# An attention and mixture-of-experts kernel: one-hot routing rows by comparing logits with the two largest, and q and k rotated in one VectorE operation

## The chip, the cores and the metric

The kernel runs on one core of one Trainium2 chip. The metric is the device time of one execution in microseconds (us). The profile shows five engines of that core: PE (TensorE: matmuls, with PEld for its weight loads), DVE (VectorE), ACT (ScalarE), POOL (GpSimd) and SP (SyncE, which here only issues DMA transfers). Each engine takes its instructions in the order in which they stand; engines wait for each other through semaphores.

## The reference

```python
def _attn_ref(q, k, v, a_re, a_im):            # B=4, H=8, S=768, D=48
    mag = np.sqrt(a_re * a_re + a_im * a_im)
    scale = np.minimum(mag, 0.999) / (mag + 1e-06)
    a_re_n, a_im_n = (a_re * scale, a_im * scale)
    for t in range(S):                         # complex state S, D x D per head
        S_re, S_im = (ar * S_re - ai * S_im + kv, ar * S_im + ai * S_re)
        y[:, :, t] = einsum('bhd,bhde->bhe', q[:, :, t], S_re)

def _moe_ref(x, w_gate, w_noise, noise, w1, w2):   # N=3072, D=384, E=8, F=1024
    noisy_logits = x @ w_gate + np.log1p(np.exp(x @ w_noise)) * noise
    top2 = np.argpartition(-noisy_logits, 2, axis=1)[:, :2]
    top2_w = softmax over the two logits
    out[row] = sum over its two experts e of weight * (relu(x @ w1[e]) @ w2[e])
```

The output of the attention, put in rows of 384, is the input x of the mixture of experts.

## The kernel before, in words

**Attention.** The sequence is cut into 24 tiles of 128 positions (6 stretches g of the sequence times 4 batches b). The decay of the state is taken out of the recurrence: its magnitude multiplies q and k (line 280, `qk` by `ee`), its phase turns them. `p3q` does the turning for one tile: q (i = 0) and k (i = 1) are each multiplied by the cosine and the sine rows `tr`, in one operation of 768 elements per partition each (line 288), into `qh` and `kh`. There are two buffers of each (`NQ = 2`), so tile n+2 writes over tile n. Then `tr_unit` transposes the eight heads of q, later those of k, on PE into the one PSUM tile `ptr` (line 298), and ACT copies them out as `qT` and `kT` (line 299); `sc_unit` makes the scores `psc` in two halves (307) and DVE masks each into `am` (308); `st_unit` adds k times v to the state in `pG` (317), which reads `kh` directly; `y_unit` makes the output `pY` from state and scores (354, 356), which ACT copies to `xT` (357).

**Gating.** `gate_logits` makes the logits of a group of tiles, `gates` turns them into weights: `softplus`, the eight largest logits of each row sorted (`max`, line 57, one for each tile), the positions of these (`max_index`, line 59, which the trace shows as MATCH_VALUE_LOAD and FIND_INDEX8), one-hot rows `oh` by comparing the positions with 0 to 7 (line 61), softmax weights. `gate_dispatch` counts the rows of each expert on PE (405, 407, from `ohs`, line 400) and POOL scatters each row to its slots (421). The groups are four of 4 tiles (`ga4`), two of 3 (`ga3`) and two of 1 (`ga1`).

**Experts.** Eight experts follow with w1 and w2 split in high and low parts (`load_w1`, `load_w2`, 494, 495), `mm1` (557, 559, 563) and `mm2` (606, 617), whose results POOL scatters (618). A flag says whether the fast way was valid; where it was not, slower code (`slow_attention`, `dense_experts`) runs instead.

**Order.** Each unit is given a step by hand (the table `P` and `at`); within that priority a scheduler places the instructions on the engines, so a change of one operation can move others.

Of the kernel before, what the change touches and what calls it, by code (L numbers as in the profile page):

```python
# [9 lines left out]
F32 = mybir.dt.float32  # L10
F32R = mybir.dt.float32r
BF16 = mybir.dt.bfloat16
U32 = mybir.dt.uint32
I32 = mybir.dt.int32
AF = mybir.ActivationFunctionType
OP = mybir.AluOpType
AX = mybir.AxisListType
# [27 lines left out]
    return c  # L45


def gates(nc, pool, lz, noise, iota8, n, tag, act, g):


    nl = softplus(nc, pool, lz[:, :, 8:16], [128, n, 8], tag, act)
    nc.vector.tensor_mul(nl, nl, noise)
    nc.vector.tensor_add(nl, nl, lz[:, :, 0:8])
    mx = pool.tile([128, n, 8], F32, name=tag + "mx")
    ix = pool.tile([128, n, 8], U32, name=tag + "ix")
    for j in range(n):
        nc.vector.max(mx[:, j, :], nl[:, j, :])
    for j in range(n):
        nc.vector.max_index(ix[:, j, :], mx[:, j, :], nl[:, j, :])
    oh = pool.tile([128, 2, n, 8], F32, name=tag + "oh")  # L60
    nc.vector.tensor_tensor(oh, iota8[:, None, None, :].to_broadcast([128, 2, n, 8]),
                            ix[:, :, 0:2, None].rearrange("p n k o -> p k n o").to_broadcast([128, 2, n, 8]),
                            op=OP.is_equal)
    w = pool.tile([128, 2, n], F32, name=tag + "w2")
    e = pool.tile([128, n], F32, name=tag + "e")
    nc.vector.tensor_sub(e, mx[:, :, 1], mx[:, :, 0])
    act(w[:, 1], e, AF.Exp)
    nc.vector.tensor_scalar(e, w[:, 1], 1.0, 1e-9, op0=OP.add, op1=OP.add)
    nc.vector.reciprocal(w[:, 0], e)
    nc.vector.tensor_mul(w[:, 1], w[:, 1], w[:, 0])  # L70
    t = pool.tile([128, 2, n, 8], F32, name=tag + "t")
    nc.vector.tensor_mul(t, oh, w[:, :, :, None].to_broadcast([128, 2, n, 8]))
    nc.vector.tensor_add(g, t[:, 0], t[:, 1])
    return oh
# [3 lines left out]
def kernel(  # L78
# [8 lines left out]
    nc = tc.nc  # L87
# [3 lines left out]
    D = HD // H  # L91
    N, DM = out.shape
    E = w_gate.shape[1]
# [6 lines left out]
    NQ = 2  # L100
# [38 lines left out]
    iota8 = cp.tile([128, E], F32, name="iota8")  # L139
    nc.gpsimd.iota(iota8, pattern=[[1, E]], base=0, channel_multiplier=0,  # L140
                   allow_small_or_imprecise_dtypes=True)
    base_run = cp.tile([128, E], F32, name="base_run")
# [21 lines left out]
    pa = ap.enter_context(tc.tile_pool(name="pa", bufs=1, side="right"))  # L164
# [9 lines left out]
    nc.gpsimd.memset(wg, 0.0)  # L174
    nz = cp.tile([128, NG, B, E], F32, name="nz")

    qh = [pa.tile([128, H, 2, 64], F32, name=f"qh{i}") for i in range(NQ)]
    kh = [pa.tile([128, H, 2, 64], F32, name=f"kh{i}") for i in range(NQ)]
    for t in qh + kh:
        nc.gpsimd.memset(t[:, :, :, D:], 0.0)  # L180
    ecol = [pa.tile([112, B, H], F32, name=f"ecol{i}") for i in range(3)]
    for t in ecol:
        nc.vector.memset(t, 1.0)
# [7 lines left out]
    QT, KT, AM, Z, XR, QKD = {}, {}, {}, {}, {}, {}  # L191
# [91 lines left out]
        for r in range(2):  # L283
            nc.sync.dma_start(ec[64 * r:64 * r + D, b, :], es[n].rearrange("(h d) -> d h", h=H))

    def p3q(n, i):
        tr = TR[n // 2][:, :, n % 2, :].rearrange("p r (h d) -> p r h d", h=H)
        nc.vector.tensor_mul((qh, kh)[i][n % NQ][:, :, :, 0:D].rearrange("p h r d -> p r h d"),
                             QK[n][:, i, :].rearrange("p (h d) -> p h d", h=H)[:, None].to_broadcast([128, 2, H, D]),
                             tr)  # L290

    def tr_unit(n, i):
        x = (qh, kh)[i][n % NQ]
# [100 lines left out]
    def gate_dispatch(g, lo, hi, lz):  # L394
        n = hi - lo
        oh = gates(nc, pa, lz, nz[:, g, lo:hi], iota8, n, f"ga{n}",
                   lambda *a: phase(2 * min(g + 3, NG), *a),
                   XR[g][:, lo:hi, DM:DM + E])
        ohs = pa.tile([128, n, E], BF16, name=f"ohs{n}")
        nc.vector.tensor_add(ohs, oh[:, 0], oh[:, 1])  # L400
        p = psC.tile([128, 512], F32, name="cum")
        for j in range(n + 1):
            o = p[:, j * E:(j + 1) * E]
            for i in range(min(j, n)):
                nc.tensor.matmul(o, ones_b, ohs[:, i, :], start=(i == 0), stop=(j == n and i == n - 1))
            if j < n:
                nc.tensor.matmul(o, tri_b, ohs[:, j, :], start=(j == 0), stop=True)
        pos = pa.tile([128, n, E], F32, name=f"pos{n}")
        nc.vector.tensor_add(pos, p[:, :n * E].rearrange("p (b e) -> p b e", b=n),
                             base_run[:, None, :].to_broadcast([128, n, E]))  # L410
        nc.vector.tensor_add(base_run, base_run, p[:, n * E:(n + 1) * E])
        if g == NG - 4:
            nc.vector.tensor_copy(ncnt, base_run[:, 0:2])
        nc.vector.tensor_mul(oh, oh, pos[:, None].to_broadcast([128, 2, n, E]))
        sl = pa.tile([128, 2, n], U32, name=f"sl{n}", bufs=2)
        with nc.allow_low_precision("whole numbers"):
            nc.vector.tensor_reduce(sl, oh, axis=AX.X, op=OP.add)
        nc.sync.dma_start(xd[(g * B + lo) * C:(g * B + hi) * C].rearrange("(b s) r -> s b r", b=n), XR[g][:, lo:hi, 0:DM + E])
        for b in range(n):
            for kk in range(2):  # L420
                d = nc.gpsimd.indirect_dma_start(  # L421
                    out=xs, out_offset=bass.IndirectOffsetOnAxis(ap=sl[:, kk, b:b + 1], axis=0),
                    in_=XR[g][:, lo + b, :], in_offset=None, bounds_check=E * N - 1, oob_is_err=False)
                for s in scat:
                    tc.declare_no_dep(d.ins, s.ins, reason="slots differ")
                scat.append(d)

                n_y = PACE.get((g, lo + b))
                if n_y is not None:
                    behind.append((d, n_y))  # L430
# [4 lines left out]
    def at(step, f, *a):  # L435
        fill.setdefault(step, []).append((f, a))
# [190 lines left out]
    for g in range(NG):  # L627
        f = B * g + .5
        q1, q2, q3 = P.get(f"s{g}", (P["p1"], P["p2"], P["p3"]))
        for j in range(B // 2):  # L630
            m = B * g // 2 + j
            at(f - P["la"] if g else -20, load_a, m)
            at(f - q1 + j * P["d1"], p1, m)
            at(f - q2, p2a, m)
            at(f - q2, p2carry, m)
            at(f - q2 + .01, p2s, m)
        for j in range(B):
            n = B * g + j
            at(f - P["lqk"] if g else -14, load_qk, n)
            at(f - q2 + j * P["dt"], p2t, n)  # L640
            at(f - q3 + j * P["d3"] if n > 1 else f - q2 - .25, p3, n)
            for i in range(2):
                at(n + .5 - P["q"] + i * P["qd"] if n > 1 else f - q3, p3q, n, i)
    for n in range(NT):
        at(n + .5 - P["lv"], load_v, n)
        for i in range(2):
# [99 lines left out]
    nc.vector.tensor_add(ncnt[:, 0:1], ncnt[:, 0:1], ncnt[:, 1:2])  # L746
    flg = mp.tile([128, 2], F32, name="flg")
    nc.vector.tensor_reduce(flg[:, 0:1], bad.rearrange("p x g -> p (x g)"), axis=AX.X, op=OP.add)
    nc.vector.tensor_reduce(flg[:, 1:2], lim, axis=AX.X, op=OP.add)
    nc.vector.tensor_add(flg[:, 1:2], flg[:, 1:2], flg[:, 0:1])  # L750
    nc.vector.tensor_add(flg[:, 1:2], flg[:, 1:2], ncnt[:, 0:1])
# [196 lines left out]
```

## Time and profile before

| what | value |
|---|---|
| median of 3 runs | 720.92 us (720.32 to 721.93) |
| profiled execution: own time | 721.25 us |
| its span, first to last instruction | 719.5 us |
| PE busy | 668.2 us (93%) |
| DVE busy | 411.7 us (57%) |
| ACT busy | 327.6 us (46%) |
| POOL busy | 164.7 us (23%) |

The attention lies in about the first 270 us of the span, the experts behind it, with a stretch in which both are interleaved. The busy shares of DVE and ACT are means over two very different halves. The own time is the span and 1.75 us around it.

### The profile page before, as it was taken

How to read it: one execution, taken by the hardware profiler on the slowest of the kernel's cores; microseconds unless marked ns; L12 is line 12 of the kernel's file. 1: busy time of each engine (PE TensorE's matmuls, PEld its weight loads, DVE VectorE, ACT ScalarE, POOL GpSimd, SP SyncE). 2: the span in 40 equal slices, each digit the busy share in tenths (PEclk: the TensorE clock that was granted, in tenths of full speed). 3: DMA queues.
4: the chain of work that ended last, by engine and by line, in shares of the span. 5: the costliest groups of instructions: out<-in, count | busy, mean ns of one | idle time of the engine just before them, and what ended most of it. 6: DMA issues, size and time to landing. Idle time of an engine off the chain costs nothing. (4 is left out here: it accounts for less than half of the span.)

```text
span 719.5 us, 13289 instructions
## 1 busy us (share of the span) xinstructions
PE 668.2 (93%) x5120; PEld 595.9 (83%) x5120; DVE 411.7 (57%) x907; ACT 327.6 (46%) x541; POOL 164.7 (23%) x183
## 2 busy tenths in 40 slices
PE   1589999999999969999999999999999999999995
PEld 0367787978788958988898999899899899899895
DVE  6788899999988637454326424624624524524311
ACT  6679989797954523333205214413413413413300
POOL 2000002232411244101422221411412412412311
PEclk9879999999999987999999999999999999999999
DMA  7477776753373436414326215415404604602201
GB/s 266 113 238 213 252 203 231 207 176 94 134 195 137 152 136 224 148 52 162 94 87 220 79 60 183 141 69 176 141 26 145 217 23 155 204 23 67 64 22 45
DMA packets 63902, 100.24 MB, mean 139 GB/s; under 512 B 26264, under 2 KB 45989, under 8 KB 63824
## 3 DMA queue, kind: packets, MB, share of 16 engines
q1 hardware_dynamic: 54464, 71.68, 32.3%
q0 software_dynamic: 9360, 27.54, 10.9%
q8 instruction: 46, 0.75, 0.5%
q14 instruction: 32, 0.26, 0.1%
HBM read 68.55 MB, written 31.69 MB: 139 GB/s over the span
## 5 line engine op out<-in xcount | busy, mean ns | idle before, releaser
L606 PE MATMUL po<-w2h,h 128*128 128x384 f32 x768 | 205.3, 340 | 2.1 <-DVE ao L617 2.1
L557 PE MATMUL ph<-x,w1h 128*128 128x512 f32 (+2 forms) x720 | 187.5, 348 | 1.4 <-DVE h L563 1.0
L606 PEld LDWEIGHTS po<-w2h,h 128*128 128x128 f32 x768 | 140.4, 189 | 3.7 <-DVE ao L617 3.6
L557 PEld LDWEIGHTS ph<-x,w1h 128*128 128x128 f32 x720 | 125.7, 189 | 19.2 <-DVE h L563 1.8
L606 PE MATMUL po<-w2l,h 128*128 128x384 f32 x384 | 129.1, 336 | 0.0
L557 PE MATMUL ph<-x,w1l 128*128 128x512 f32 (+2 forms) x360 | 124.4, 346 | 0.0
L618 POOL DMA_INDIRECT out_dram<-ao,ox x52 | 51.0, 981 | 270.2 <-DVE ao L617 238.4
L563 DVE SCALAR_TENSOR_TENSOR h<-ph,h 128x512 fp32r<-128x512 f32 (+2 forms) x144 | 70.0, 506 | 70.3 <-ACT h L559 59.0
L559 ACT ACTIVATE h<-ph 128x512 fp32r<-128x512 f32 (+2 forms) x120 | 60.3, 509 | 103.1 <-PE ph L557 84.8
L617 DVE SCALAR_TENSOR_TENSOR ao<-po,gw,ao 128x384 f32<-128x384 f32 (+1 forms) x52 | 31.9, 613 | 125.6 <-PE po L606 125.3
L421 POOL DMA_INDIRECT xs<-xr,sl x48 | 53.0, 1104 | 215.7 <-ACT t L200 103.8
L538 ACT CAST x<-px 128x512 fp32r<-128x512 f32 (+1 forms) x42 | 21.4, 519 | 125.6 <-PE px L533 125.6
L557 PEld LDWEIGHTS ph<-x,w1l 128*128 128x128 f32 x360 | 68.0, 189 | 7.8
L606 PEld LDWEIGHTS po<-w2l,h 128*128 128x128 f32 x384 | 72.8, 189 | 0.1
L582 POOL DMA_INDIRECT ao<-out_dram,ox x49 | 54.2, 1106 | 51.0 <-DMA out_dram<-ao,ox 31.9
L307 PE MATMUL psc<-qT,kT 112*128 112x128 f32 x384 | 52.1, 281 | 0.0
L307 PEld LDWEIGHTS psc<-qT,kT 112*128 112x128 f32 x384 | 48.1, 195 | 2.5 <-issue 1.2
L356 PE MATMUL pY<-am,v 128*48 128x128 f32 x384 | 41.9, 275 | 1.5 <-DVE am L308 1.4
L494 ACT CAST w2h<-raw 128x768 fp32r<-128x768 f32 x32 | 26.4, 835 | 32.8 <-PE po L606 17.2
L495 DVE TENSOR_TENSOR w2l<-raw,w2h 128x768 fp32r<-128x768 f32 x32 | 30.5, 958 | 14.5 <-ACT w2h L494 13.5
L298 PE MATMUL ptr<-ident,qh 128*112 128x128 f32 x192 | 30.1, 289 | 8.6 <-ACT kT L299 7.9
L354 PE MATMUL pY<-qT,z 112*48 112x128 f32 x320 | 36.0, 274 | 1.1 <-ACT xT L357 0.9
(210 smaller groups left out, 950.8 us busy)
## 6 DMA issues: line engine op xcount, KB each, us to landing
raw<-in_moe_w_dram SPq DMA_DIRECT2D x24, 512.0 KB
raw<-in_moe_w_dram SPq DMA_DIRECT2D x32, 384.0 KB
qk<-in_qk_dram SPq DMA_DIRECT2D x24, 384.0 KB
xgb<-xs SPq DMA_DIRECT2D x8, 800.0 KB
re<-in_a_dram SPq DMA_DIRECT2D x12, 384.0 KB
im<-in_a_dram SPq DMA_DIRECT2D x12, 384.0 KB
v<-in_v_dram SPq DMA_DIRECT2D x24, 192.0 KB
out_dram<-zero SPq DMA_DIRECT2D x12, 384.0 KB
```

The source lines that it names most:

```text
L307: nc.tensor.matmul(p[:, j, :], KT[n][:, h, :], QT[n][:, h, :], start=True, stop=True)
L354: nc.tensor.matmul(o, Z[b][:, h, :], QT[n][:, h, :], start=True, stop=False, skip_group_check=True)
L356: nc.tensor.matmul(o, V[n][:, h, :], AM[n][:, h, :], start=not g, stop=True, skip_group_check=True)
L421: d = nc.gpsimd.indirect_dma_start(out=xs, out_offset=bass.IndirectOffsetOnAxis(ap=sl[:, kk, b:b + 1], axis=0), in_=XR[g][:, lo + b, :], i ...
L495: d = nc.vector.tensor_tensor(lo, raw_t, hi.bitcast(F32), op=OP.subtract)
L557: LAST['m'] = nc.tensor.matmul(p[:, :c], W1[e, kk][i][:, f * 128:(f + 1) * 128], XW[w, kk][:, j, 0:c], start=(m == 0), stop=(m == len(ms) ...
L559: nc.scalar.activation(h[:, 0:c], p[:, :c], AF.Relu)
L563: LAST['h'] = nc.vector.scalar_tensor_tensor(h[:, dst:dst + b - a], p[:, a:b], 0.0, h[:, a:b].bitcast(F32), op0=OP.max, op1=OP.subtract)
L582: nc.gpsimd.indirect_dma_start(out=ao[j][0:w, :], out_offset=None, in_=out, in_offset=bass.IndirectOffsetOnAxis(ap=OX[e][0:w, j:j + 1], ax ...
L606: LAST['po'] = nc.tensor.matmul(p[:, :DM], HT[w, f][i][:, o:o + 128], W2[f // 2][k2][:, f % 2, :], start=(m == 0), stop=(m == len(ms) - 1))
L617: nc.vector.scalar_tensor_tensor(a, p[0:n, :DM], g, a, op0=OP.mult, op1=OP.add)
L618: nc.gpsimd.indirect_dma_start(out=out, out_offset=bass.IndirectOffsetOnAxis(ap=OX[e][0:n, j:j + 1], axis=0), in_=a, in_offset=None, bound ...
```

## The change

The two operations of `p3q` become one of 1,536 elements per partition that writes q and k of a tile into a common tile `qkh`; there are two such tiles in place of two and two. In `gates` the fast way compares the logits themselves with the two largest ones, so that `max_index` is left out; a row with equal logits would then have more than two ones. Three small DVE operations ahead of the flag add up the counts of all experts and set the flag where the sum is not the expected one. `slow_attention` keeps the positions (`ties=True`). New line numbers are 5 to 8 higher than old ones.

```diff
-def gates(nc, pool, lz, noise, iota8, n, tag, act, g):
+def gates(nc, pool, lz, noise, iota8, n, tag, act, g, ties=True):
...
     for j in range(n):
         nc.vector.max(mx[:, j, :], nl[:, j, :])
-    for j in range(n):
-        nc.vector.max_index(ix[:, j, :], mx[:, j, :], nl[:, j, :])
     oh = pool.tile([128, 2, n, 8], F32, name=tag + "oh")
-    nc.vector.tensor_tensor(oh, iota8[:, None, None, :].to_broadcast([128, 2, n, 8]),
-                            ix[:, :, 0:2, None].rearrange("p n k o -> p k n o").to_broadcast([128, 2, n, 8]),
+    if ties:
+        ix = pool.tile([128, n, 8], U32, name=tag + "ix")
+        for j in range(n):
+            nc.vector.max_index(ix[:, j, :], mx[:, j, :], nl[:, j, :])
+        a, b = iota8[:, None, :].to_broadcast([128, n, 8]), ix
+    else:
+
+        a, b = nl, mx
+    nc.vector.tensor_tensor(oh, a[:, None].to_broadcast([128, 2, n, 8]),
+                            b[:, :, 0:2, None].rearrange("p n k o -> p k n o").to_broadcast([128, 2, n, 8]),
                             op=OP.is_equal)
...
-    qh = [pa.tile([128, H, 2, 64], F32, name=f"qh{i}") for i in range(NQ)]
-    kh = [pa.tile([128, H, 2, 64], F32, name=f"kh{i}") for i in range(NQ)]
-    for t in qh + kh:
-        nc.gpsimd.memset(t[:, :, :, D:], 0.0)
+    qkh = [pa.tile([128, 2, H, 2, 64], F32, name=f"qkh{i}") for i in range(NQ)]
+    for t in qkh:
+        nc.gpsimd.memset(t[:, :, :, :, D:], 0.0)
+    qh, kh = ([t[:, i] for t in qkh] for i in range(2))
...
-    def p3q(n, i):
+    def p3q(n):
         tr = TR[n // 2][:, :, n % 2, :].rearrange("p r (h d) -> p r h d", h=H)
-        nc.vector.tensor_mul((qh, kh)[i][n % NQ][:, :, :, 0:D].rearrange("p h r d -> p r h d"),
-                             QK[n][:, i, :].rearrange("p (h d) -> p h d", h=H)[:, None].to_broadcast([128, 2, H, D]),
-                             tr)
+        nc.vector.tensor_mul(qkh[n % NQ][:, :, :, :, 0:D].rearrange("p i h r d -> p r i h d"),
+                             QK[n].rearrange("p i (h d) -> p i h d", h=H)[:, None].to_broadcast([128, 2, 2, H, D]),
+                             tr[:, :, None].to_broadcast([128, 2, 2, H, D]))
...
-            for i in range(2):
-                at(n + .5 - P["q"] + i * P["qd"] if n > 1 else f - q3, p3q, n, i)
+            at(n + .5 - P["q"] if n > 1 else f - q3, p3q, n)
...
+    tot = mp.tile([128, 1], F32, name="tot")
+    nc.vector.tensor_reduce(tot, base_run, axis=AX.X, op=OP.add)
+    nc.vector.tensor_scalar(tot, tot, float(2 * N + N * E * (E - 1) // 2), None, op0=OP.not_equal)
+    nc.vector.tensor_add(flg[:, 0:1], flg[:, 0:1], tot)
```

The change moves instructions. On DVE, at the start of the attention (rotations of the first four tiles), before:

```order
L288 TENSOR_TENSOR qh_124<-qk,tr 128x2x8x48
L260 TENSOR_TENSOR tf<-tf,cum 128x384
L288 TENSOR_TENSOR kh_126<-qk,tr 128x2x8x48
L267 TENSOR_SCALAR tf<-tf 128x768
L288 TENSOR_TENSOR qh_125<-qk,tr 128x2x8x48
L288 TENSOR_TENSOR kh_127<-qk,tr 128x2x8x48
L329 COPY z_482<-pG 112x384
L329 COPY z_555<-pG 112x384
L280 TENSOR_TENSOR qk<-qk,ee 128x768 x2
```

and in the change:

```order
L293 TENSOR_TENSOR qkh_124<-qk,tr 128x2x16x48
L265 TENSOR_TENSOR tf<-tf,cum 128x384
L293 TENSOR_TENSOR qkh_125<-qk,tr 128x2x16x48
L272 TENSOR_SCALAR tf<-tf 128x768
L334 COPY z_476<-pG 112x384
L334 COPY z_548<-pG 112x384
L285 TENSOR_TENSOR qk<-qk,ee 128x768 x2
```

Here `tf` of line 260 (265) now stands behind q and k of the first tile, where it stood behind q alone, and `tf` of line 267 (272) behind both of the second tile.

On PE, in the second stretch g of the sequence (buffers 124 and 126 are q and k of even tiles, 125 and 127 of odd ones), before:

```order
L356 MATMUL pY<-am,v 48x128 x2
L298 MATMUL ptr<-ident,qh_125 112x128 x8
L307 MATMUL psc<-qT,kT 128x128 x8
L298 MATMUL ptr<-ident,kh_127 112x128 x8
L317 MATMUL pG<-v,kh_126 48x48 x16
L354 MATMUL pY<-qT,z_639 48x128 x2
```

and in the change (the first `ptr` of `qkh_125` is q, the second is k):

```order
L361 MATMUL pY<-am,v 48x128 x2
L312 MATMUL psc<-qT,kT 128x128 x2
L303 MATMUL ptr<-ident,qkh_125 112x128 x8
L312 MATMUL psc<-qT,kT 128x128 x6
L303 MATMUL ptr<-ident,qkh_125 112x128 x8
L322 MATMUL pG<-v,qkh_124 48x48 x16
L359 MATMUL pY<-qT,z_631 48x128 x2
```

The transposes of the next tile's q moved behind two of the eight score matmuls of the tile at hand.

On DVE, behind the first gating (its last row `sl` first), before:

```order
L417 TENSOR_REDUCE sl_994<-ga4oh 128x8
L308 TENSOR_TENSOR am<-psc,mask 128x512
L246 SCALAR_TENSOR_TENSOR t_1089<-car,t_1089 1x768
L246 SCALAR_TENSOR_TENSOR t_1184<-car,t_1184 1x768
L326 TENSOR_TENSOR z_775<-z_775,pG 112x384
L288 TENSOR_TENSOR qh_125<-qk,tr 128x2x8x48
L257 SCALAR_TENSOR_TENSOR tf<-tf,cum 128x384 x2
L337 TENSOR_TENSOR fcol<-ecol_133,ecol_134 112x32
L288 TENSOR_TENSOR kh_127<-qk,tr 128x2x8x48
```

and in the change:

```order
L422 TENSOR_REDUCE sl_978<-ga4oh 128x8
L239 SCALAR_TENSOR_TENSOR t_1165<-t_1165,t_1166 128x768
L313 TENSOR_TENSOR am<-psc,mask 128x512
L293 TENSOR_TENSOR qkh_125<-qk,tr 128x2x16x48
L241 SCALAR_TENSOR_TENSOR t_1165<-t_1165,t_1166 128x768
L251 SCALAR_TENSOR_TENSOR t_1073<-car,t_1073 1x768
L251 SCALAR_TENSOR_TENSOR t_1167<-car,t_1167 1x768
L331 TENSOR_TENSOR z_766<-z_766,pG 112x384
```

The rotation of q and k now stands right behind the mask `am`, ahead of the carries and of the state's addition; before, q and k stood behind these and apart.

## Rows read from the trace of the kernel before

**Rows 1.** The head of the page: the span, and of each engine its busy time in us, its share of the span and its instructions.

```profile
span 719.5 us, 13289 instructions
...
PE 668.2 (93%) x5120; PEld 595.9 (83%) x5120; DVE 411.7 (57%) x907; ACT 327.6 (46%) x541; POOL 164.7 (23%) x183
```

**Rows 2.** Busy time of each engine by stretches of the span: stretch, its length, busy us of PE, PEld, DVE, ACT, POOL (with the instructions), mean granted clock of PE as a share of full speed, DMA share, GB/s.

```profile
20.00:60.00 40.00, 30.13 (x271) 21.78 (x270) 32.30 (x49) 31.01 (x45) 0.00 (x0) 0.83 0.61 180
60.00:222.00 162.00, 156.51 (x1960) 129.98 (x1958) 152.13 (x353) 134.48 (x218) 31.72 (x32) 1.00 0.63 190
222.00:262.00 40.00, 40.00 (x406) 36.06 (x405) 24.90 (x95) 20.02 (x37) 9.29 (x9) 1.00 0.37 126
262.00:280.00 18.00, 9.59 (x48) 8.14 (x47) 8.58 (x40) 5.75 (x12) 8.66 (x10) 0.62 0.48 163
280.00:719.00 439.00, 428.05 (x2437) 398.13 (x2435) 182.31 (x346) 123.50 (x213) 109.81 (x107) 1.00 0.34 112
```

**Rows 3.** What PE waited for in the stretch from 60 to 222 us, those rows that name DVE with 0.4 us or more for attention and gating: us in total, times, longest.

```profile
PE cum L251 <- DVE t L246: 0.9, 2, 0.7
...
PE cum L407 <- DVE ohs L400: 0.7, 2, 0.5
PE pY L356 <- DVE am L308: 0.4, 1, 0.4
```

**Rows 4.** Groups of DVE instructions by line and shape: line, operation, out<-in, shapes, count | busy us, mean ns of one | idle us of DVE before them and what ended it.

```profile
L288 DVE TENSOR_TENSOR kh<-qk,tr 128x768 f32<-128x768 f32 x24 | 22.8, 951 | 2.5 <-PE pG L317 2.5
...
L59 DVE FIND_INDEX8 ga4ix<-ga4mx,ga4c 128x8 uint32<-128x8 f32 x16 | 2.3, 160 | 0.0
...
L59 DVE MATCH_VALUE_LOAD ga4ix<-ga4mx,ga4c 128x8 f32 x16 | 1.2, 72 | 0.0
...
L750 DVE TENSOR_TENSOR flg<-flg 128x1 f32<-128x1 f32 x1 | 0.1, 150 | 0.0
```

**Rows 5.** DVE in order of time, at the rotations of the first two tiles: start us, duration us, instruction.

```profile
24.91 0.96 DVE L288 TENSOR_TENSOR qh<-qk,tr 128x768 f32<-128x768 f32 x1
25.79 0.55 DVE L260 TENSOR_TENSOR tf<-tf,cum 128x384 f32<-128x384 f32 x1
26.25 0.95 DVE L288 TENSOR_TENSOR kh<-qk,tr 128x768 f32<-128x768 f32 x1
27.12 0.55 DVE L267 TENSOR_SCALAR tf<-tf 128x768 int32<-128x768 int32 x1
27.59 0.95 DVE L288 TENSOR_TENSOR qh<-qk,tr 128x768 f32<-128x768 f32 x1
28.46 0.95 DVE L288 TENSOR_TENSOR kh<-qk,tr 128x768 f32<-128x768 f32 x1
```

**Rows 6.** ACT in order of time, from the same place on (in brackets: idle us before it, and what ended it).

```profile
26.37 0.85 ACT L200 ACTIVATE tr<-tf 128x768 f32<-128x768 f32 x1 [1.49 <-DVE tf L260]
...
28.68 0.93 ACT L200 ACTIVATE tr<-tf,b_cos 128x768 f32<-128x768 f32 x1
...
35.52 1.04 ACT L299 ACTIVATE kT<-ptr 112x1024 f32<-112x1024 f32 x1
```

**Rows 7.** PE in order of time: its two longer waits behind this place.

```profile
36.61 1.96 PE L298 MATMUL ptr<-ident,qh 128*112 128x128 f32 x8 [5.76 <-ACT kT L299]
...
46.33 0.43 PE L298 MATMUL ptr<-ident,qh 128*112 128x128 f32 x2 [1.19 <-ACT kT L299]
```

**Rows 8.** DVE in order of time at the gating of four tiles: the first of the four pairs of `max_index`, and the instruction behind the last.

```profile
204.91 0.07 DVE L59 MATCH_VALUE_LOAD ga4ix<-ga4mx,ga4c 128x8 f32 x1
...
205.45 0.15 DVE L66 TENSOR_TENSOR ga4e<-ga4mx 128x4 f32<-128x4 f32 x1
```

**Rows 9.** All engines in order of time around one tile's state update: the state's matmuls, the output's, k's rotation for a later tile, and the transposes of its q.

```profile
202.10 0.93 PE L317 MATMUL pG<-v,kh 128*48 128x48 f32 x32
202.86 0.39 PE L354 MATMUL pY<-qT,z 112*48 112x128 f32 x4
...
203.08 0.96 DVE L288 TENSOR_TENSOR kh<-qk,tr 128x768 f32<-128x768 f32 x1 [0.51 <-PE pG L317]
...
204.72 1.08 PE L298 MATMUL ptr<-ident,qh 128*112 128x128 f32 x8
```

**Rows 10.** All engines in order of time at the end of the attention: the last output matmuls, the three `max` of the gating, the one count matmul, what followed, and matmuls of the first expert (L606) early and later. The word remote stands where a semaphore ended the wait and no recorded instruction ends at that time.

```profile
261.67 0.39 PE L356 MATMUL pY<-am,v 128*48 128x128 f32 x4
...
262.09 0.31 DVE L57 MAX8 ga3mx<-ga3c 128x8 f32<-128x8 f32 x3
...
263.32 0.18 PE L407 MATMUL cum<-ohs,tri_b 128*128 128x8 bf16 x1 [0.78 <-DVE ohs L400]
...
270.13 0.60 ACT L357 ACTIVATE xT<-pY 128x512 f32<-128x512 f32 x1 [8.73 <-remote]
...
270.79 1.12 PE L364 MATMUL cum<-ident,xT 128*128 128x128 f32 x4 [7.28 <-ACT xT L357]
...
276.61 0.84 PE L606 MATMUL po<-w2h,h 128*128 128x384 f32 x2
...
277.57 0.84 PE L606 MATMUL po<-w2h,h 128*128 128x384 f32 x2
...
279.43 0.51 PE L606 MATMUL po<-w2h,h 128*128 128x384 f32 x2
...
279.96 0.51 PE L606 MATMUL po<-w2h,h 128*128 128x384 f32 x2
```

More of the change, by code (lines that the diff above doesn't have):

```diff
@@ L54, in gates @@
     mx = pool.tile([128, n, 8], F32, name=tag + "mx")
-    ix = pool.tile([128, n, 8], U32, name=tag + "ix")
     for j in range(n):
         nc.vector.max(mx[:, j, :], nl[:, j, :])
-    for j in range(n):
-        nc.vector.max_index(ix[:, j, :], mx[:, j, :], nl[:, j, :])
     oh = pool.tile([128, 2, n, 8], F32, name=tag + "oh")
-    nc.vector.tensor_tensor(oh, iota8[:, None, None, :].to_broadcast([128, 2, n, 8]),
-                            ix[:, :, 0:2, None].rearrange("p n k o -> p k n o").to_broadcast([128, 2, n, 8]),
+    if ties:
[7 more added lines that the diff above has]
+                            b[:, :, 0:2, None].rearrange("p n k o -> p k n o").to_broadcast([128, 2, n, 8]),
                             op=OP.is_equal)
@@ L397, in gate_dispatch @@
                    lambda *a: phase(2 * min(g + 3, NG), *a),
-                   XR[g][:, lo:hi, DM:DM + E])
+                   XR[g][:, lo:hi, DM:DM + E], ties=False)
         ohs = pa.tile([128, n, E], BF16, name=f"ohs{n}")
```

## The prediction

> **What bounds the kernel now.** I read the head of the page first, then the busy time by stretches, then PE's waits, and last the order of time at the places where PE stands still. The head [rows 1] gives PE 93% of the span and DVE 57%. The change takes work from DVE alone, so the question is where DVE still decides when PE may go on. The stretches [rows 2] answer most of it. From 280 us on PE works 428.05 of 439 us while DVE works 182.31: DVE is hidden there, and this is over half of the time. From 222 to 262 PE is busy without a gap. From 60 to 222 both are nearly full (PE 156.51 of 162, DVE 152.13), so PE has 5.5 us of idle time to give back, and no more. From 20 to 60 PE works 30.13 of 40, waiting on a chain of DVE and ACT. From 262 to 280 it works 9.59 of 18.
>
> Two stops stand out. One is at 36.61, where PE waited 5.76 us for ACT's `kT` [rows 7]. The other, the longest behind the start, is at 270.79: 7.28 us for ACT's `xT` [rows 10]. There ACT itself waited 8.73 us, released by something that the trace doesn't name, although the output matmuls that it needs began at 261.67 and should have ended near 262.1. Its cause isn't readable here; I come back to it as a rival.
>
> **The change part by part.** *Removed: the positions.* Four pairs of MATCH_VALUE_LOAD and FIND_INDEX8 run from 204.91 to 205.45 [rows 8], 0.135 us a pair; singly they last 72 and 160 ns [rows 4], but they overlap. There is one pair a tile, so 24 pairs or 3.2 us of DVE. The comparison that remains has the shape it had. The work that hides this is PE's own between 60 and 222. PE waited for DVE in the three rows of this kind 0.9 + 0.7 + 0.4 = 2.0 us in all [rows 3]; that is the most that relief can bring here, and the least is nothing. At the last groups PE waited 0.78 us for `ohs` [rows 10], which three pairs fewer shorten by 0.4; then it runs into the 7.28 us wait, which swallows that.
>
> *Merged: the rotation.* Back to back, 768 elements take 28.46 - 27.59 = 0.87 us and 384 take 26.25 - 25.79 = 0.46 [rows 5], so 0.41 us for 384 more. 1,536 elements are then 0.87 + 2 x 0.41 = 1.69 us where the pair took 1.74. An operation ends 0.08 after the next begins, so the merged one ends 1.77 us after its start. It saves 0.05 us a tile, 1.2 us in all, if the strides cost nothing; the trace shows no operation of this size.
>
> Alone an operation of 768 elements lasts 0.951 us [rows 4], against 0.87 in a row. [...]
>
> *Later q.* q used to be ready 0.96 us after the start and now is after 1.77, 0.81 later; k is no later. At the start nothing hides this. The order shows q and k of the first tile ahead of `tf` (line 260), so `tf` begins at 26.60, not 25.79, and ACT, which waited for it at 26.37 [rows 6], starts 0.8 later. PE's transposes of q are 0.8 late too, so are ACT's copy of them and its cosine at 28.68. From there ACT is busy up to `kT` at 35.52, for which PE waits at 36.61. So PE restarts near 37.4. Behind that, DVE wins time back: the rotation of the fourth tile, whose q stood ahead of the next logarithm's products, now stands behind both masks, 0.87 us that are no longer in the way. ACT's next waits for DVE come earlier by that, its copies for PE don't. Of the 0.8 I let half reach 46.33, where PE waits for `kT` again: **0.4 us**, bounds 0 and 0.8. Behind 46 PE is nearly full, so it is carried on.
>
> *The common buffer.* The ring of two now frees q and k together: the merged operation of tile n+2 must wait for the state matmuls of tile n, which read k; q alone had only to wait for its own transposes. Queued behind it on DVE are the carries and the addition of the state (third place of the order), and PE's next transposes wait for it. In one tile [rows 9] the state matmuls give way to the output at 202.86, k's rotation begins at 203.08 when they have ended, and q's transposes begin at 204.72. A merged operation begun at 203.08 ends at 204.85; 0.13 late, and up to 0.9 later where DVE has just begun another of 0.95 us. Against that the scheduler put two score matmuls ahead of those transposes. Bounds: nothing, and 16 tiles of the full stretch at 0.3 on average, near 5 us. The case read here is 0.13 late, with such cover about even, so I take 0 to 0.3 and balance it with the gain from relief above: **0**.
>
> *Added: the check of the counts.* Three small DVE operations at 0.15 to 0.2 each (the like of L750, 150 ns [rows 4]), 0.5 us, among the first experts. DVE is under half busy there [rows 2]; PE has products to do meanwhile. Nothing. Without that cover it would be 0.5 us. The two POOL fills in place of four come while PE has no input yet. The scheduler's orders behind the attention are otherwise alike.
>
> **The sum.** The profiled execution took 721.25 us; with 0.4 from the start and 0 from the rest it would be 721.65. The runs have their median at 720.92, 0.33 below that execution, so I forecast **721.3 us**, no change: a measurement of this kernel tells about 0.2% (1.4 us) from none.
>
> **The rivals.** *The stop at 262 us goes away* (faster). For it: what ACT waited for had finished on PE's side by all rows, and the stop begins while DVE does its run of short operations, three `max` at 262.09 and three pairs behind them [rows 10], of which the pairs go. A lost or late signal could depend on just that. Against it: four groups of four tiles have longer runs and no such stop. It would give 7.28 us at least. [...] Time: 721.3 - 7.3 - 3.9 = 710.1, or 714.0 if the clock falls anyway.
>
> [...]
>
> *The full stretch tightens* (slower). For it: DVE is 94% busy there, waited 2.5 us for the state matmuls before k [rows 4], and now holds back q with it. From about nine tiles that lose 0.13 it is 1.2 us and decides, 722.5; at the 5 us above, 726.3.
>
> *Relief counts* (faster): PE's 2.0 us of waits go, 719.3. Against it: DVE gives back only 3.2 + 1.2 us spread over the whole attention, and part of these waits is for chains through ACT.
>
> *A second stop like that at 262* (slower): 7 us or more, 729.
>
> **How the numbers follow.** No change 0.38; the stop gone 0.24; tightening 0.25; relief 0.08; a second stop 0.05. Faster: 0.24 + 0.08 = 0.32. Same 0.38. Slower: 0.25 + 0.05 = 0.30. Around the likeliest alone the range is 719.9 to 722.4, with 0.8 of start either way and the balance of two small terms. For 8 in 10 both neighbours must be in: from 709.5, the stop and its clock gone, to 725, most of the tightening; left out are the second stop, the worst of the tightening, and a gain beyond 11 us.
>
> **What would show it.** A merged rotation of 1.75 us alone, 24 times; no MATCH_VALUE_LOAD. PE's wait near 36.6 ending near 37.4, the one near 46.3 near 46.7. PE idle from 60 to 222 still about 5.5 us; if it grows, with waits of `ptr` for the rotation, the ring is the cause. The stop for `xT` at the attention's end still about 7 us. I am wrong if that stop is gone, or if DVE's waits for `pG` double and PE's follow.

## The result and the profile after

The changed kernel takes **728.29 us** (median of 4 runs, 726.02 to 729.18) against 720.62 us for the kernel before on the same chip (4 runs, 719.37 to 721.93): a ratio of **1.0096** [1.0075, 1.0117], slower by about 7 us. The forecast of 721.3 us and its range up to 725.0 were both too low. The profiled execution took 727.96 us, 1.7 of it outside the span.

The head of the page as in [rows 1], the group of the merged rotation as in [rows 4], and the busy time of two stretches as in [rows 2], of the changed kernel:

```profile
span 726.3 us, 13208 instructions
...
PE 672.8 (93%) x5120; PEld 598.8 (82%) x5120; DVE 407.7 (56%) x838; ACT 327.8 (45%) x541; POOL 170.5 (23%) x181
...
L293 DVE TENSOR_TENSOR qkh<-qk,tr 128x1536 f32<-128x1536 f32 x24 | 42.1, 1754 | 2.7 <-PE cum L369 1.3 <-PE pG L322 1.2
...
60.00:222.00 162.00, 156.45 (x1898) 129.16 (x1897) 144.20 (x292) 134.26 (x217) 34.24 (x31) 0.99 0.59 182
...
262.00:280.00 18.00, 10.82 (x111) 8.20 (x107) 6.15 (x27) 5.57 (x13) 7.80 (x8) 0.81 0.31 114
```

DVE's work fell by 4.0 us as forecast, and PE's busy time rose by 4.6. From 60 to 222 PE is idle for 5.55 us as before, but issued 1,898 matmuls where it had issued 1,960: it lost ground while it was busy, in part at a lower granted clock (0.99 on the mean, before 1.00). So stretches of fixed time hide this loss. A mark in the work shows it: the start of ACT's copy of a tile's attention output (`xT<-pY`), and of the first `po` matmul behind the attention.

| mark | before, us | after, us | later by |
|---|---|---|---|
| tile 0 | 46.18 | 49.72 | 3.5 |
| tile 6 | 103.07 | 105.54 | 2.5 |
| tile 8 | 122.44 | 127.93 | 5.5 |
| tile 22 | 256.53 | 262.35 | 5.8 |
| first `po` | 275.82 | 283.17 | 7.4 |
| end | 719.5 | 726.3 | 6.8 |

Three places lose, then: the start, the tiles from 6 to 8, and the end of the attention.

**The start.** DVE, ACT and PE of the changed kernel in order of time, the counterpart of [rows 5 to 7], and the granted clock (the number after the five engines) from 27 to 30 us:

```profile
25.65 1.76 DVE L293 TENSOR_TENSOR qkh<-qk,tr 128x1536 f32<-128x1536 f32 x1
27.33 0.55 DVE L265 TENSOR_TENSOR tf<-tf,cum 128x384 f32<-128x384 f32 x1
27.79 1.75 DVE L293 TENSOR_TENSOR qkh<-qk,tr 128x1536 f32<-128x1536 f32 x1
...
27.56 1.29 PE L303 MATMUL ptr<-ident,qkh 128*112 128x128 f32 x5 [1.48 <-DVE qkh L293]
28.64 1.48 PE L280 MATMUL cum<-t,tri_l 128*128 128x384 f32 x2
29.92 0.84 PE L303 MATMUL ptr<-ident,qkh 128*112 128x128 f32 x3
...
39.75 1.93 PE L303 MATMUL ptr<-ident,qkh 128*112 128x128 f32 x8 [5.93 <-ACT kT L304]
...
38.57 1.04 ACT L304 ACTIVATE kT<-ptr 112x1024 f32<-112x1024 f32 x1
...
27.00:30.00 3.00, 2.44 (x8) 1.74 (x9) 3.00 (x4) 0.84 (x1) 0.00 (x0) 0.58 0.88 260
```

The same stretch of the kernel before:

```profile
27.00:30.00 3.00, 2.65 (x47) 2.00 (x47) 2.88 (x5) 2.45 (x4) 0.00 (x0) 1.00 0.86 254
```

The first rotation begins 0.74 us later than in [rows 5]; that is no part of the change (in e1 below, with the old rotations, it begins at 25.55). PE restarts at 39.75 where it was 36.61 [rows 7], so 2.4 us are the change's own. PE has waited 1.48 us for the longer rotation, and while it then transposes q, the granted clock is 0.58 on the mean from 27 to 30 us, and 0.50 from 28 to 30.

**Tiles 6 to 8.** PE's wait for the carry (`car`, the angles summed up so far) of the third group, DVE ahead of it, and the stretch around it:

```profile
112.07 1.75 DVE L293 TENSOR_TENSOR qkh<-qk,tr 128x1536 f32<-128x1536 f32 x1
113.74 0.95 DVE L241 SCALAR_TENSOR_TENSOR t<-t,t 128x768 f32<-128x768 f32 x1
114.71 1.82 DVE L251 SCALAR_TENSOR_TENSOR t<-car,t 1x768 f32<-1x768 f32 x2
...
115.71 2.44 PE L256 MATMUL cum<-t,tri_t 128*128 128x384 f32 x4 [1.99 <-DVE t L251]
...
112.00:120.00 8.00, 6.01 (x37) 4.41 (x36) 7.32 (x13) 6.08 (x9) 2.35 (x2) 0.79 0.86 305
```

A rotation of 1.75 us stands ahead of the last polynomial step (line 241) of a chain for which PE waits 1.99 us. The granted clock is 0.79 on the mean from 112 to 120, where before it was 1.00.

**The end of the attention.** The stop of [rows 10] is still there, 6.12 us for ACT and 4.77 for PE:

```profile
273.40 0.60 ACT L362 ACTIVATE xT<-pY 128x512 f32<-128x512 f32 x1 [6.12 <-remote]
...
274.05 1.12 PE L369 MATMUL cum<-ident,xT 128*128 128x128 f32 x4 [4.77 <-issue]
```

### The profile page after: what moved, and what is told of

Same layout as the page of the kernel before. It is cut to its first block, busy times and chain, and to the rows that moved or that the text cites. A ratio compares the mean times of both kernels' runs of the same rounds, so it can differ in the third digit from the quotient of the medians.

```text
span 726.3 us, 13208 instructions
## 1 busy us (share of the span) xinstructions
PE 672.8 (93%) x5120; PEld 598.8 (82%) x5120; DVE 407.7 (56%) x838; ACT 327.8 (45%) x541; POOL 170.5 (23%) x181
## 5 line engine op out<-in xcount | busy, mean ns | idle before, releaser
L426 POOL DMA_INDIRECT xs<-xr,sl x48 | 56.4, 1174 | 216.7 <-DMA out_dram<-zero 105.9
L303 PE MATMUL ptr<-ident,qkh 128*112 128x128 f32 x384 | 56.0, 284 | 11.1 <-ACT kT L304 9.3
L303 PEld LDWEIGHTS ptr<-ident,qkh 128*112 128x112 f32 x384 | 44.8, 138 | 19.5 <-issue 11.5
L312 PE MATMUL psc<-qT,kT 112*128 112x128 f32 x384 | 54.8, 285 | 0.0
L293 DVE TENSOR_TENSOR qkh<-qk,tr 128x1536 f32<-128x1536 f32 x24 | 42.1, 1754 | 2.7 <-PE cum L369 1.3
```

The source lines that it names most:

```text
L293: nc.vector.tensor_mul(qkh[n % NQ][:, :, :, :, 0:D].rearrange("p i h r d -> p r i h d"), QK[n].rearrange("p i (h d) -> p i h d", h=H)[:, N ...
L303: nc.tensor.transpose(p[:, h, :], x[:, h, :, :].rearrange("p r x -> p (r x)")[:, 0:112], ident)
L312: nc.tensor.matmul(p[:, j, :], KT[n][:, h, :], QT[n][:, h, :], start=True, stop=True)
L426: d = nc.gpsimd.indirect_dma_start(out=xs, out_offset=bass.IndirectOffsetOnAxis(ap=sl[:, kk, b:b + 1], axis=0), in_=XR[g][:, lo + b, :], i ...
```

## Experiments

The chips on which the experiments ran fall into two kinds. On some the kernel before takes 720.6 to 721.7 us, on two others 710.5 to 710.9. So each run is given as a ratio to the kernel before on its own chip. It lies up to 0.2% from the ratio of the two medians; the interval is at 95%.

| run | gating | rotation | buffers | ratio | interval |
|---|---|---|---|---|---|
| the change | new | merged | 2 | 1.0096 | 1.0075 to 1.0117 |
| c_after | new | merged | 2 | 1.0117 | 1.0094 to 1.0141 |
| e1 | new | two operations | 2 | 0.9989 | 0.9973 to 1.0004 |
| e2 | old | merged | 2 | 1.0068 | 1.0051 to 1.0085 |
| e4 | new | merged from the fifth tile on | 2 | 1.0094 | 1.0077 to 1.0111 |
| e5 | new | merged in the first four tiles | 2 | 1.0021 | 1.0003 to 1.0040 |
| e7 | new | two operations, order of the change | 2 | 1.0185 | 1.0143 to 1.0226 |
| e8 | new | merged, order of e1 | 2 | 1.0254 | 1.0231 to 1.0276 |
| e6 | new | two operations that wait as one | 2 | 1.0050 | 1.0024 to 1.0076 |
| h3 | new | as e4, written 0.25 of a tile earlier | 2 | 1.0063 | 1.0038 to 1.0087 |
| i1 | new | as e4, 0.05 later | 2 | 1.0101 | 1.0074 to 1.0128 |
| h4 | new | as e4, 1 earlier (computes something else) | 2 | 0.9999 | 0.9984 to 1.0014 |
| e9 | new | as e4 | 3 | 0.9985 | 0.9966 to 1.0004 |
| e11 | new | two operations, 0.25 earlier | 2 | 1.0005 | 0.9985 to 1.0024 |
| e10 | new | two operations | 3 | 1.0074 | 1.0049 to 1.0099 |
| i2 | new | as e10, 0.25 earlier | 3 | 1.0017 | 0.9999 to 1.0035 |
| h1 | new | as e1, last x earlier | 2 | 0.9963 | 0.9942 to 0.9984 |
| h2 | new | as e9, last x earlier | 3 | 0.9939 | 0.9916 to 0.9963 |

### Each half alone, and the start against the rest

```diff
 e1: gates(..., ties=False) and the check of the counts; qh, kh and their two operations as before
 e2: qkh and the merged operation; gates as before, no check of the counts
 e4: (e5 with n < 4)
+            if n > 3:
                 at(n + .5 - P["q"] if n > 1 else f - q3, p3q, n)
+            else:
+                for i in range(2):
+                    at(n + .5 - P["q"] + i * P["qd"] if n > 1 else f - q3, p3qi, n, i)
```

e1: 

> Gating by comparison alone; q and k rotated in two operations as before. Theory A, the whole loss of 7.5 us comes with the merged rotation: 720.6 as before, at most 0.7 either way (DVE loses 3.2 us of work that PE hides). Theory B, the loss comes with the gating (other order of the last groups, other run of short operations ahead of the stop): 724 to 728. The stop for xT at the attention's end: 7 us by A if it hangs on the scatters, gone if it hung on the position pairs.

e2: 

> Merged rotation alone; gating by positions as before. Theory A: 727 to 729, with the first tile's attention output about 3 us late and the eighth's 5 to 6 us late, as in the changed kernel. Theory B: 721 to 724.

e4: 

> The changed kernel, with the first four tiles rotated in two operations and the other twenty merged. Theory A1, the start is a term of its own (PE gets the first tiles' q late, +2 to +3.5 us, and the rest is lost between the sixth and the eighth tile): 725 to 726. Theory A2, what the start loses is made up by then, and all is lost behind: 728. Theory A3, the late start is the cause of all that follows: 720 to 721.

e5: 

> The counterpart: the first four tiles merged, the other twenty in two operations. A1: 722.6 to 724. A2: 720.6. A3: 727 to 729.

The gating alone changes nothing (0.9989). The rotation alone costs 0.68%, less than theory A's 0.9 to 1.2% and more than theory B's 0.5%: most of the loss comes with it. At tile 22 e2 is as late as c_after below, on another chip of its kind (262.45 against 262.06); c_after then loses 1.8 us more up to the first `po` (274.48, in e2 273.03), by a wait that comes with the new gating (last section of the experiments).

e5 costs 0.32% more than e1 by the ratios, 1.8 us by the medians (712.81 against 710.98). Its marks run 2.0 us behind e1's from tile 1 to tile 22, to 0.1. e4 costs 1.05% more than e1, 6.2 us by the medians (717.22). So the twenty later tiles cost three times what the start does; A1 is right that the start is a term of its own; its size for e4 (4.4 to 5.4 us over the kernel before, measured 6.3) was too small.

Marks of two executions also differ by what is no part of an edit. From tile 0 to tile 1 e1 takes 13.8 us, e4 and e5 take 12.2: from 46 to 50 us e1's granted clock is 0.68, theirs is 1.00. At tile 0 e5 is 3.6 us behind e1, of which 0.8 is a later first rotation.

e4 has the order of e1 in the first four tiles, so the two can be laid side by side at the third group's angles. DVE and PE of e1:

```profile
93.51 0.95 DVE L293 TENSOR_TENSOR qh<-qk,tr 128x768 f32<-128x768 f32 x1
...
105.55 0.95 DVE L293 TENSOR_TENSOR kh<-qk,tr 128x768 f32<-128x768 f32 x1
106.78 0.96 DVE L241 SCALAR_TENSOR_TENSOR t<-t,t 128x768 f32<-128x768 f32 x1
109.48 1.80 DVE L251 SCALAR_TENSOR_TENSOR t<-car,t 1x768 f32<-1x768 f32 x2
...
99.93 0.93 PE L322 MATMUL pG<-v,kh 128*48 128x48 f32 x32
102.54 1.08 PE L303 MATMUL ptr<-ident,qh 128*112 128x128 f32 x8
...
110.56 1.56 PE L256 MATMUL cum<-t,tri_t 128*128 128x384 f32 x4
```

And of e4:

```profile
101.62 1.75 DVE L293 TENSOR_TENSOR qkh<-qk,tr 128x1536 f32<-128x1536 f32 x1
108.16 1.75 DVE L293 TENSOR_TENSOR qkh<-qk,tr 128x1536 f32<-128x1536 f32 x1
109.83 0.95 DVE L241 SCALAR_TENSOR_TENSOR t<-t,t 128x768 f32<-128x768 f32 x1
110.80 1.81 DVE L251 SCALAR_TENSOR_TENSOR t<-car,t 1x768 f32<-1x768 f32 x2
...
111.80 2.63 PE L256 MATMUL cum<-t,tri_t 128*128 128x384 f32 x4 [1.99 <-DVE t L251]
```

In e1 q of tile 8 is rotated at 93.51, 9 us before PE transposes it at 102.54, and before the group's chain of angles; it need not wait for the state matmuls of tile 6, which read k until 100.86. In e4 the merged operation must, and begins at 101.62. So between 95 and the carry DVE does 0.95 us of rotation in e1 and 3.5 in e4, among the operations of the chain. PE waits 1.99 us, and e4's granted clock from 112 to 120 is 0.79, e1's 1.00. e4 was 1.9 us ahead at tile 6 (101.64 against 103.55; by its first rotation and the clock from 46 to 50) and is 1.7 behind at tile 8.

### The same chip for both, and the order against the operation

c_before and c_after are the two kernels unchanged. In e7 and e8 the order of every engine is a table up to the end of the attention:

```diff
+ORDER = {"tensor": "0-7 ...", "vector": "...", ...}
+    for e, rows in ORDER.items():
+        for x, y in zip(seq, seq[1:]):
+            tc.add_manual_dep(ISSUED[e][y].ins, ISSUED[e][x].ins.name, after, reason="order")
 e7: the order of the change
+        for i in range(2):
+            nc.vector.tensor_mul((qh, kh)[i][n % NQ]..., QK[n][:, i, :]..., tr)
 e8: the order of e1, the merged operation in the first place that k's readers leave it
```

c_before: 

> The kernel before once more, for its trace on the same chip as the next three. If the stop for xT at the attention's end (7.3 us) belongs to the kernel, it is there again and the time is near 720; if it belongs to some chips alone, the time is near 711 without it, as its runs beside the first four kernels were (710.9).

c_after: 

> The changed kernel once more. If its loss has nothing to do with that stop, it takes 0.8 to 1.1% more than the kernel before, whatever chip (717 to 719 where the kernel before takes 711), and the stop is there or not there in both.

e7: 

> The changed kernel's order of instructions, engine by engine and written out as a table, but each merged rotation split again into its two operations, one right behind the other. Theory O, the new order by itself costs the time (the scheduler places the longer operation that waits for more elsewhere, and other work with it): 0.8 to 1.1% above the kernel before, as the changed kernel. Theory L, the length of the merged operation costs it (q 0.8 us later in each tile): at most 0.3% above, since q is early again.

e8: 

> The counterpart: merged rotations in the order of the kernel with gating alone (711.0, 0.1% below the kernel before), each in the first place on DVE at which, by that kernel's trace, k's readers of two tiles earlier have ended; for six tiles that is within 1 us of PE's transposes of q. Theory O: the start's 1.5 us and about 2 us of those six tiles, 0.2 to 0.5% above the kernel before. Theory L: 0.8% or more above.

c_before took 711.9 us in its one run (span 710.1) and c_after 719.46: here neither kernel has the stop, and the change costs 1.17%. ACT's copy and POOL's ninth scatter in a row of c_after (start, length, idle time before), and its wait for the carry:

```profile
267.64 0.60 ACT L362 ACTIVATE xT<-pY 128x512 f32<-128x512 f32 x1 [0.71 <-PE pY L361]
...
276.16 0.97 POOL L426 DMA_INDIRECT xs<-xr,sl  x1 [0.30 <-issue]
...
117.43 1.56 PE L256 MATMUL cum<-t,tri_t 128*128 128x384 f32 x4 [1.99 <-DVE t L251]
...
112.00:120.00 8.00, 5.80 (x54) 4.47 (x52) 7.97 (x14) 7.50 (x11) 2.70 (x2) 1.00 1.01 345
```

Its marks stand 2.5 us behind c_before's at tile 0, 3.9 at tile 6, 6.3 at tile 22, 8.1 at the first `po`, and 8.5 at the end. The loss has nothing to do with the stop. In c_after PE also waits 2.0 us for the carry, and the clock stays at 1.00 from 112 to 120: the fall there is not certain, the wait is.

e7 ends theory L: two operations in the new order are no faster than one. They are 0.67% slower than c_after, although the start is theirs again (tile 0 at 47.66, against 49.74); at tile 22 they stand 2.0 us behind. That is past theory O's 1.1% too; what such a table itself costs is not shown, as no kernel ran with its own order in one. But e8 ends theory O as well: the merged operation in the old order is the slowest of all, 2.65% over e1. Its waits from 60 to 262 us, the two longest rows (a helper issues every operation there, so all have its line):

```profile
PE cum L171 <- DVE ohs L171: 5.2, 4, 2.3
PE cum L171 <- DVE t L171: 2.5, 2, 1.3
```

So the new order alone is not what spoils the change. It is the scheduler's better answer to an operation that waits longer and then blocks DVE longer. But it has a price of its own. From the mark of tile 8 to that of tile 22 PE runs the same matmuls in one sequence in e1 and e8, and in another in e4, e7 and the change. The stretch between these marks, columns as in [rows 2], in e1, e8, e4 and e7:

```profile
122.30:253.10 130.80, 129.66 (x1611) 112.48 (x1610) 113.67 (x285) 96.11 (x163) 34.59 (x36) 1.00 0.53 162
126.99:267.19 140.20, 130.61 (x1611) 112.47 (x1610) 114.68 (x271) 96.25 (x163) 36.42 (x36) 1.00 0.49 151
124.03:258.06 134.03, 133.71 (x1611) 114.22 (x1610) 112.17 (x270) 95.96 (x163) 40.54 (x36) 1.00 0.51 158
126.48:264.09 137.61, 135.27 (x1611) 115.54 (x1610) 112.81 (x283) 95.88 (x163) 41.78 (x36) 0.99 0.49 153
```

In the old sequence these 1,611 matmuls keep PE busy for 129.7 and 130.6 us, in the new one for 133.7 and 135.3, whichever operation rotates. e8 pays for the merged operation in idle time (9.6 us), e4 in the sequence: it is idle for less than e1 (0.3 against 1.1) and still loses 3.2 us here.

e8 also parts the two costs of the start. Its first rotation is merged and begins at 25.59. PE and ACT of e8, with the granted clock, and ACT of e1 (rotation at 25.55):

```profile
27.49 0.73 PE L171 MATMUL ptr<-ident,qkh 128*112 128x128 f32 x5 [1.48 <-DVE qkh L171]
...
27.00:30.00 3.00, 2.51 (x42) 1.97 (x42) 2.96 (x4) 1.61 (x2) 0.00 (x0) 1.00 0.62 177
...
37.00 1.04 ACT L171 ACTIVATE kT<-ptr 112x1024 f32<-112x1024 f32 x1
...
36.16 1.04 ACT L304 ACTIVATE kT<-ptr 112x1024 f32<-112x1024 f32 x1
```

PE waits 1.48 us as in the changed kernel, but the granted clock stays at 1.00, and `kT` comes 11.41 us after the rotation's start: 0.80 more than in e1, where the changed kernel needs 12.92.

What neither table takes away is the binding itself: q waits for k's readers.

### The binding

```diff
 e6, from the fifth tile on, two operations, and
+        for t in TRS[n - 2][H:] + STS.get(n - 2, []):
+            tc.add_manual_dep(ROT[n, 0].ins, t.ins.name, later, reason="pair")
+        for t in TRS[n][:H]:
+            tc.add_manual_dep(t.ins, ROT[n, 1].ins.name, later, reason="pair")
 e9 on e4, e10 on e1
-    NQ = 2
+    NQ = 3
 both, for room: bufs of v 6 -> 4, of xT 6 -> 5, zero = none[:, 0:DM]
 e11 on e1: q=2 -> q=2.25
```

e6: 

> Gating by comparison, two operations per tile in the common buffer, the scheduler free to order them; but from the fifth tile on q's operation is made to wait for k's readers of two tiles earlier, and PE's transposes of q for k's operation, as if both were one. Theory B, binding q to k is what costs (q was rotated up to 12 us before k's readers let the merged operation begin, and so filled DVE's quiet times): 0.4 to 1.1% above the kernel before, near the kernel with the first four tiles apart (0.94%). Theory L, the length of the merged operation: within 0.2%.

e9: 

> The kernel with the first four tiles apart and the other twenty merged (0.94% above), with three common buffers in place of two, so that the merged operation waits for readers of three tiles earlier; room is made by fewer buffers of v (4 of 6) and of the transposed output (5 of 6), which alone leaves the order of PE, DVE and ACT as it was. Theory B: the loss goes, 0.3% below to 0.2% above. Theory L or any theory that blames the merged operation itself: 0.6 to 1.1% above.

e10: 

> The control with three buffers and two operations per tile. Every theory: as with gating alone (0.1% below) or up to 0.3% faster.

e11: 

> Gating alone with the rotations written a quarter of a tile earlier, which makes the scheduler place some 700 of 5,000 PE instructions elsewhere without any new wait. Theory S, any other order of the scheduler's moves the time by half a per cent either way, and the change met a bad one: more than 0.4% from the kernel before. Theory B: within 0.3%.

Binding two operations costs 0.61% over e1 (e6), and 0.45% over e11 on the same chip. With a third buffer twenty merged operations cost nothing (e9: tile 22, which lies ahead of the stop, at 253.56; e1's at 253.10, e4's at 258.06). Both as theory B says. e11 has another order without a binding and stays at 1.0005. e10 fits nothing: no binding, one buffer more, and 0.74% slower. Its longest wait between the marks of tile 8 and tile 22 is 1.2 us; the stretch:

```profile
121.91:260.17 138.26, 134.71 (x1611) 113.42 (x1610) 112.37 (x284) 95.87 (x162) 35.77 (x36) 1.00 0.50 154
```

So it met a sequence in which PE's matmuls take 5 us longer than e1's, and PE is idle for 2.4 us more. The order that the scheduler happens to find can be worth 0.7% without any binding, and one more question was whether the bound kernels had only met bad ones.

### Other orders with and without the binding

```diff
 h3, h4, i1 on e4: q=2 -> q=2.25, q=3, q=1.95
 i2 on e10: q=2 -> q=2.25
```

h3: 

> Twenty merged rotations in two buffers (0.94% above), written a quarter of a tile earlier: another order of some 800 of 5,000 PE instructions with the same bindings. Theory B: 0.4 to 1.3% above again. Theory S, it is only the order that was met: anywhere from 0.2% below to 1.3% above, and with h4 at least one within 0.2%.

h4: 

> The same, written a whole tile earlier (another 800 PE instructions elsewhere). Theory B: 0.4 to 1.3% above. Theory S: see h3.

i1: 

> Twenty merged rotations in two buffers (0.94% above; 0.63% when written a quarter of a tile earlier), written 0.05 of a tile later: a third order, some 940 of 5,000 PE instructions elsewhere, all bindings kept. Theory B: 0.4 to 1.3% above. Theory S: anywhere from 0.5% below to 1.3% above.

i2: 

> Two operations per tile with three buffers (0.74% above, which theory B did not foresee), written a quarter of a tile earlier: another order of some 780 PE instructions, no binding. If the 0.74% was that one order: within 0.3% of the kernel before. If three buffers and two operations are slow in any order: 0.5 to 1.0% above.

h4 is not the run it was meant to be. A whole tile earlier, the rotation of tile n is written ahead of the state matmuls of tile n - 2, which then read the k of tile n. That part of the computation is changed, and with it the wait for these matmuls is gone, which is most of the binding. By its expectation alone it would speak for theory S; I count its 0.9999 for neither, and i1 took its place. The three orders that keep the binding cost 0.94, 0.63 and 1.01%. Of the kernels without it (in e9 it is loosened) four lie between 0.15% below and 0.17% above (e9, e11, i2, e1), and e10 alone at 0.74%. PE is busy from tile 8 to tile 22 for 132.4 to 133.7 us in the three, for 129.4 to 132.2 in the four. The binding costs 0.5 to 1% in every order that the scheduler found with it; why it found e10's order is not explained, and i2 shows that it was that one order.

### The end of the attention

The gating alone gains 2.7 us up to tile 22 (253.10, in c_before 255.78; from tile 8 on PE is idle for 1.1 us in place of 2.4 and busy for 1.0 less) and ends level. Where it goes is seen behind the attention. DVE and PE of e1:

```profile
261.01 1.21 DVE L500 TENSOR_TENSOR w1l<-raw,w1h 128x1024 fp32r<-128x1024 f32 x1
262.91 1.22 DVE L500 TENSOR_TENSOR w1l<-raw,w1h 128x1024 fp32r<-128x1024 f32 x1
264.33 0.48 DVE L544 TENSOR_TENSOR x<-ptr,x 128x320 fp32r<-128x320 f32 x1
...
264.96 0.52 PE L538 MATMUL ptr<-ident,xga 128*128 128x128 f32 x3 [2.84 <-DVE ga1c L43]
...
262.00:272.00 10.00, 6.34 (x25) 5.89 (x25) 8.96 (x34) 3.00 (x7) 8.03 (x7) 0.69 0.89 322
```

And of c_before:

```profile
264.39 1.22 DVE L495 TENSOR_TENSOR w1l<-raw,w1h 128x1024 fp32r<-128x1024 f32 x1
265.53 0.48 DVE L539 TENSOR_TENSOR x<-ptr,x 128x320 fp32r<-128x320 f32 x1
...
266.06 0.55 PE L533 MATMUL ptr<-ident,xga 128*128 128x128 f32 x3 [0.35 <-DVE x L539]
```

Without the position pairs the scheduler places two splits of `w1` ahead of the second `x`. PE waits 2.84 us for it (the row names the short operation that ended with it), and the clock falls: 0.69 from 262 to 272, in c_before 1.00. The changed kernel has the same wait, 2.85 us at 282.64; e2, with the old gating, waits 0.35 there.

```diff
 h1 on e1, h2 on e9
-xu1=22.8
+xu1=22.5
```

h1: 

> Gating alone (0.1% below the kernel before) with the transposes of the second expert's first window written 0.3 of a tile earlier, so that DVE has all three of its x behind the attention ahead of the second and third w1l of 1.22 us; nothing else in the order moves. In gating alone PE waited 2.84 us there for x, and ran at the lower clock from 265 to 272. Theory E, the gating's gain in the middle (2.6 us) is lost again at that place: 0.3 to 0.9% below the kernel before. If another wait takes its place: as gating alone, within 0.15%.

h2: 

> The same edit in the kernel with twenty merged rotations and three common buffers (0.15% below). Theory E: 0.4 to 1.0% below the kernel before.

Both are theory E: h1 0.26% under e1, h2 0.46% under e9. The wait is gone; on this chip the stop stands at these transposes instead (PE waits 5.9 us there in h1, 6.0 in h2). The edit also moved matmuls that it was to leave alone: from tile 8 to tile 22 h1 takes 133.3 us, e1 130.8. **h2 beats both kernels**: 716.28 us where the kernel before takes 721.53.

## Why the prediction was wrong

- **Positions removed** (0, at most 2.0): the 0 came out (0.9989), but by luck. e1 gains 2.7 us up to tile 22 and then loses it behind the attention. Of the gain 1.3 us are idle time of PE, within the 2.0 that I counted, the rest lies in PE's order. I had costed the removal by DVE's time alone and had taken the scheduler's orders behind the attention as alike; the step that failed is "alike", two `w1l` ahead of `x`.
- **The merged operation**: 1.68 us to the next start (25.65 to 27.33) and 1.76 to its end, forecast 1.69 and 1.77. Alone a pair would be 2 x 0.951 = 1.90, and it is 1.754, a gain of 0.15. As forecast, the shorter time buys nothing.
- **Later q at the start** (0.4, at most 0.8): it was 1.8 to 2.4. The latency was right: PE's transposes begin 1.91 us after the rotation's start, in e1 1.10 (25.55 to 26.65), 0.81 later. The step that failed is "0.8 later in all that follows": PE's wait grew to 1.48 us, the granted clock fell, and its ten matmuls up to the last transpose of q took 3.20 us (27.56 to 30.76), in e1 1.71 (26.65 to 28.36). That is 1.49 more, and 0.81 + 1.49 = 2.3 is what `kT` is late by (38.57 against 35.52 in [rows 6], less the 0.74). In e8, where the clock did not fall, `kT` was the forecast 0.8 late.
- **The common buffer** (0, bounds 0 to 5): with the order that came with it, it costs 6.2 us by the medians and 7.5 by the ratios, as e4 against e1 has it. I priced it by how late q would reach PE in [rows 9], 0.13 us. The q that PE transposes there at 204.72 had been rotated 13 us earlier, as this line of the kernel before shows:

```profile
191.76 0.95 DVE L288 TENSOR_TENSOR qh<-qk,tr 128x768 f32<-128x768 f32 x1
```

The step that failed is this price: it asks when q is ready and puts at nothing that DVE's work moves from a quiet time to one behind the state matmuls, and that PE's order moves with it. At the third group of e4 1.75 us of rotation twice stand in a chain for which PE waits, which with the clock is 3.6 us from tile 6 to tile 8; PE's order is 3.2 us from there to tile 22. My upper bound of sixteen tiles at 0.3 knew nothing of either.

- **The check of the counts** (0): three operations of 147 to 159 ns (lines 754 to 756) among the experts, as forecast.
- **The rivals.** The one that came true is "the full stretch tightens" (0.25), with its sign and place, but past its worst price, and by another mechanism than tiles that each wait 0.13 us. "The stop goes away" was priced rightly, 710.1: the kernel before takes 710.5 to 710.9 where it is absent. No run shows its 3.9 us for the lower clock by themselves: c_before, without the stop and on another chip, has a span of 710.1 us where the kernel before has 719.5, and a granted clock of 1.00 from 262 to 272 where that has 0.68. But the stop does not hang on the removed pairs; with 24 pairs fewer the stop is there, and c_before and c_after, on one chip, are both without it.
- **What would show it.** PE idle from 60 to 222 stayed at 5.5 us and DVE's waits for `pG` before a rotation fell from 2.5 [rows 4] to 1.2. By my own tests the stretch had not tightened. They were the wrong tests: a lower clock and a slower order of matmuls cost time while PE counts as busy (from 60 to 222 it is busy for 156.45 us with 1,898 matmuls, before for 156.51 with 1,960).

**Open.** Why PE's matmuls took longer in one order than in another, no row tells. That the binding drives the scheduler to such orders is argued from three orders with it and four without, against which e10 stands; why the scheduler found e10's order wasn't found.

## What to carry to other kernels

When two operations become one, list what each waits for and how early each was run, not only what each costs: the merged one starts at the later of the two (e4: at 101.62, where e1 has q at 93.51) and blocks the engine for nearly the sum (1.754 us, where each alone takes 0.951). If a ring is in between, give it one more buffer together with the merge (e9 0.9985, e4 1.0094). Compare in more than one order, since an order alone was worth 0.7% in e10. Measure progress by marks in the work rather than by idle time in fixed windows, and look at the granted clock behind each wait that grows (0.58 behind the 1.48 us at the start).

## What the runs showed of the hardware

**A wait cost PE more than its length in some executions.** After a wait of 1.48 us at the start of the changed kernel the granted clock was 0.58 from 27 to 30 us, where it was 1.00 in the kernel before and in e1, without that wait; in e8, with the same wait, it was 1.00 too. After the 1.99 us at the carry it was 0.79 (112 to 120) in the changed kernel and 1.00 in c_after, the same program. What decides it, these runs don't show.

**The same matmuls took PE longer in one order than in another.** 1,611 of them kept it busy for 129.7 and 130.6 us in one sequence (e1, e8) and for 133.7 and 135.3 in another (e4, e7), at a granted clock of 1.00 (in the last 0.99).

**The stop at the attention's end came on some chips and not on others.** On chips where the kernel before takes 720.6 to 721.7 us it is in the traces of the kernel before, the change, e6, e9, e10, e11, h1, h2 and h3 (PE waits between 3.4 us in e11 and 7.7 in e6); on the two where that takes 710.5 to 710.9 it is in none of e1, e2, e4, e5, c_before, c_after, e7 and e8. In the kernel before and in the changed one POOL halts as well, after the eighth scatter in a row, for 6.90 and 8.03 us. In the changed kernel:

```profile
282.75 1.80 POOL L426 DMA_INDIRECT xs<-xr,sl  x1 [8.03 <-issue]
```

In c_after the ninth scatter follows 0.30 us after the eighth. What holds the ninth back, and ACT's copy with it, no row tells.
